# Transposes of the identity in TensorE's early waits, a higher count for x's sums in the planner, and one low part of the GLU on VectorE

## The chip, the cores and the metric

The kernel runs on one core of a Trainium2 chip. The metric is the device time of one execution in microseconds (us). TensorE (PE, with its weight loads PEld), VectorE (DVE), ScalarE (ACT) and GpSimd (POOL) each run their own queue in order; SyncE (SP) issues the DMAs.

## The reference

Three layers, in float32, over 2304 tokens of width 512:

```python
# 1. attention in chunks of 64 tokens, 8 heads of 64, softmax inside each chunk
out = softmax(q_c @ k_c.T / 8) @ v_c
# 2. x = that, heads joined; a mixture of 4 experts, F = 1024
p = domain_probs / (domain_probs.sum(-1, keepdims=True) + 1e-9)
out = sum(p[:, e:e+1] * (maximum(x @ w1[e], 0) @ w2[e]) for e in range(4))
# 3. RMS norm, then a gated unit, d_ff = 1536
xn = x / sqrt(mean(x * x) + 1e-6) * rms_g
g, val = xn @ w_gate, xn @ w_val
out = (g * sigmoid(g) * val) @ w_out
```

## The kernel before

**Tiling.** The 2304 tokens are three sets of 768; a set is two blocks of 384, a block three tiles of 128. For each layer and set the kernel walks over the feed-forward width in "outers" of two chunk pairs (`fps`, `UF = 2`). A number is held as a rounded high part and a low part, and each product is three passes (high by high, high by low, low by high). The first products (`hidden`) go by a Strassen-Winograd scheme: seven products over blocks, with sums of blocks of x (operands 4, 5, 6, 2, made by `x_sum`) and sums of blocks of the weights. Each operand is split by `x_parts`: ScalarE rounds the high part, VectorE (or GpSimd for operand 3) subtracts to get the low part. The products' sums are made on VectorE from PSUM (`u2`, `u3` and the adds into `c` and `d`).

**A GLU chunk.** `hidden` calls `use(b, j, ps)` four times, for (1,1), (0,0), (1,0) and (0,1), block b and column half j. `val_use` multiplies on VectorE, rounds `hi` on ScalarE (L734), and puts the low part's subtraction into `later`; `catch_up` issues it soon after, for (0,1) of an outer's second chunk as the first thing that `outer` does. `outer` then multiplies: tile 0 of block 0 takes (0,0) and (0,1) of both chunks, in twelve matmuls, of which the twelfth reads the low part of (0,1); block 1 follows three tiles later. There are nine outers in the GLU, so eighteen chunks, and 72 of these subtractions.

**The start.** Before the main loops, `race` writes out an order for the first attention of set 0 (three `attention_unit`s), the splitting of x, the first two chunks' products with operands 0 and 1 (`begin`, two products each, with a ScalarE copy `p1` between them, L639), and the first weights (`weights`, the `spare` runner). Each runner yields the engine and the time that its next step costs by a hand-written count; `race` always takes the runner that can begin first by these counts, and the steps go into the engines' queues in that order. So the counts decide, for example, how many of ScalarE's roundings of x's sums stand in its queue ahead of `p1`. PSUM is eight banks, handed out first in, first out.

Of the kernel before, what the change touches and what calls it, by code (L numbers as in the profile page):

```python
# [8 lines left out]
F32 = mybir.dt.float32  # L9
# [9 lines left out]
P = 128  # L19
# [52 lines left out]
class Chains:  # L72
# [28 lines left out]
                if c in self.chains and self.clock >= c[2]:  # L101
                    self.step(c, busy)

    def race(self, runners, spare):

        self.rush, busy = True, {}

        def enter(gen, at, then):
            return [gen, next(gen), [at], then]

        def begin(r):
            need, back = r[1] or ({}, 1)
            return max([r[2][-min(back, len(r[2]))]] + [busy.get(e, 0.0) for e in need])

        state, spare = [enter(*r) for r in runners], enter(*spare)
        while state:
            r = min(state, key=begin)  # L120
            if begin(spare) + 0.2 < begin(r):
                r = spare
            t, need = begin(r), (r[1] or ({}, 1))[0]
            for e, us in need.items():
                busy[e] = t + us
            r[2].append(t + max(need.values(), default=0.3) + 0.1)
            try:
                r[1] = next(r[0])
            except StopIteration:
                state.remove(r)  # L130
                state += [enter(*n) for n in (r[3](r[2][-1]) if r[3] else ())]
        self.rush = False
        self.clock = max(self.clock, busy["PE"])
        return spare[0]
# [13 lines left out]
def fused_kernel(ctx, tc, qkv, probs, w12, wglu, gvec, out):  # L148
# [4 lines left out]
    nc = tc.nc  # L153
# [13 lines left out]
    UF = 2  # L167
# [13 lines left out]
    banks = Banks(psum, [f"b{n}" for n in range(8)])  # L181
    work = Chains()

    ident = const.tile([P, P], F32, name="ident")
# [9 lines left out]
    sub = lambda eng, o, a, b: eng.tensor_tensor(o, a, b, op=ALU.subtract)  # L194
# [65 lines left out]
    def fetched():  # L260
        while not raws:
            if work.rush:
                work.step(fetching)
            yield
        ts, t = raws.pop(0)
        yield from work.pause(t + 8 - work.clock)
        return ts

    def store(t, where, name):
        yield from work.pause(3)  # L270
        nc.sync.dma_start(out=where, in_=t.bitcast(F32))
        written.add(name)
        yield from work.pause(7)
        release(t)
# [10 lines left out]
    def w1_load(where, key):  # L285
        for n in ORDER:
            while not w1p.free() or (*key[2:], n) not in written:
                yield
            t = w1p.get(f"w1_{n}")
            nc.sync.dma_start(out=t.bitcast(F32), in_=where[:, n])  # L290
            users[id(t)] = 1
            parts[(*key, n)] = t
            yield

    def weights():

        for s in range(NSET):
            for e in range(E):
                for u in range(NF1 // 2 // UF):
                    own = range(u * UF, (u + 1) * UF)  # L300
                    for fp in own if s > 0 else ():
                        yield from w1_load(w1m[e][fp], ("moe", s, e, fp))

                    for order in () if s > 0 else (ORDER,) if (e, u) != (0, 0) else ((0, 1), (5, 4, 6, 3, 2)):
                        for fp in own:
                            key, where = ("moe", s, e, fp), w1m[e][fp]
                            if order[0] == 0:
                                kept[fp] = yield from fetched()

                            def stored(n, t, key=key, where=where):  # L310
                                users[id(t)] = 2
                                parts[(*key, n)] = t
                                work.add(store(t, where[:, n], (*key[2:], n)))

                            yield from operands(kept[fp], w1p, stored, order)
                            if order[-1] == ORDER[-1]:
                                tp.put(*kept.pop(fp))
                    for f in range(2 * UF * u, 2 * UF * (u + 1)):
                        raw, = yield from fetched()
                        while not w2p.free():  # L320
                            yield
                        t = w2p.get("w2")
                        nc.scalar.copy(t[:, 0], raw)  # L323
                        yield
                        sub(nc.gpsimd, t[:, 1], raw, t[:, 0].bitcast(F32))
                        tp.put(raw)
                        parts["w2", "moe", s, e, f] = t
                        yield
        for s in range(NSET):
            for u in range(NF2 // 2 // UF):  # L330
                for fp in range(u * UF, (u + 1) * UF):
                    for g in range(2):
                        yield from w1_load(wgv[fp][g], ("glu", s, -1 - g, fp))
                for f in range(2 * UF * u, 2 * UF * (u + 1)):
                    while not w2p.free() or (f, 1) not in written:
                        yield
                    t = w2p.get("w2")
                    nc.sync.dma_start(out=t.bitcast(F32), in_=wou[f])
                    parts["w2", "glu", s, 0, f] = t
                    yield  # L340
# [216 lines left out]
    xs = {}  # L557
# [6 lines left out]
    def x_part(n, k):  # L564
        if n in tmp:
            return tmp[n][k][:, :NB]
        b, kd = x_at[n]
        return xr[:, b, kd + k, :]

    def x_sum(n):  # L570

        for o, *_ in x_made.get(n, ()):
            tmp[o] = [tp.get(f"s{o}_{k}") for k in range(KH)]
        for k in range(KH):
            for o, a, b, op in x_made.get(n, ()):
                yield {"DVE": 0.55}, 1
                op(nc.vector, x_part(o, k), x_part(a, k), x_part(b, k))

    def x_sums():
# [5 lines left out]
    def x_parts(n, eng, halves=False):  # L585

        t = xsp.tile([P, 2, KH, NB], F32R, tag=f"x{n}", name=f"x{n}")
        xs[n] = t
        if n in x_at and not halves:
            b, kd = x_at[n]  # L590
            pieces = [(slice(None), xr[:, b, kd:kd + KH, :])]
        else:
            pieces = [(k, x_part(n, k)) for k in range(KH)]
        for k, src in pieces:
            yield {"ACT": 0.5}, 1
            nc.scalar.copy(t[:, 0, k], src)
        for k, src in pieces:
            yield {"DVE": 0.55} if eng is nc.vector else {"POOL": 1.0}, len(pieces)
            sub(eng, t[:, 1, k], src, t[:, 0, k].bitcast(F32))

    def x_done():
        for n in list(tmp):
            tp.put(*tmp.pop(n))
# [15 lines left out]
    later, begun = [], {}  # L619
# [10 lines left out]
    def begin(key, use):  # L630

        yield {"PE": 1.2}, 1
        while not ((*key, 0) in parts and (*key, 1) in parts):
            yield {}, 1
        a = bank("a_ps")
        product(a, weight((*key, 0)), 0, True, False)
        yield {"ACT": 0.5}, 1
        p1 = cp.get("p1")
        nc.scalar.copy(p1, a[:, :NB])  # L639
        yield {"PE": 1.2}, 1  # L640
        product(a, weight((*key, 1)), 1, False, True)
        yield {"ACT": 0.5}, 1
        use(0, 0, a)
        yield {"DVE": 0.6}, 1
        catch_up()
        begun[key] = p1
# [80 lines left out]
    def val_use(fp):  # L727
        def use(b, j, ps):
            m = silu.pop((b, j))
            v = m[:, :NB]  # L730
            nc.vector.tensor_tensor(v, ps[:, :NB], v, op=ALU.mult)  # L731
            banks.put(ps)
            hi, lo = hh.get("hh"), hl.get("hl")
            nc.scalar.copy(hi, v)  # L734

            def rest():
                sub(nc.gpsimd, lo, v, hi.bitcast(F32))
                tp.put(m)

            later.append(rest)  # L740
            hs[fp, b, j] = (hi, lo)

        return use
# [80 lines left out]
    with tc.manual_schedule():  # L824
# [11 lines left out]
        nc.sync.dma_start(out=pr, in_=probs)  # L836
        nc.sync.dma_start(out=gb, in_=gvec.partition_broadcast(P))

        def one_block():
            yield from x_parts(0, nc.vector, True)  # L840
            yield from x_parts(1, nc.vector, True)
            for fp in range(UF):
                yield from begin(("moe", 0, 0, fp), moe_use(fp))
# [7 lines left out]
        def two_blocks(t):  # L851
            engines = {5: nc.vector, 4: nc.vector, 6: nc.vector, 3: nc.gpsimd, 2: nc.vector}
            return [(operand(n, eng), t + 0.8 * m, None) for m, (n, eng) in enumerate(engines.items())]

        gen = work.race(
            [
                (first[0], 4.4, None),
# [1 line left out]
                (first[2], 12.0, two_blocks),  # L859
            ],  # L860
            (weights(), 15.0, None),
        )
        x_done()
        feeding = work.add(gen, 0.5)
        nc.vector.tensor_reduce(psm, pr, axis=AX.X, op=ALU.add)
# [4 lines left out]
        for kind, s in [(kind, s) for kind in ("moe", "glu") for s in range(NSET)]:  # L870
            moe = kind == "moe"
# [128 lines left out]
```

## Time and profile before

| | |
|---|---|
| time, three runs | 1282.87 us median (1282.1 to 1284.8) |
| the profiled execution | 1280.6 us, span 1278.7 us |
| mean granted TensorE clock | 0.992 |
| busy share of the span | PE 96%, PEld 87%, DVE 62%, ACT 32%, POOL 44% |

TensorE is busy nearly all of the time, so the time is TensorE's work plus its idle stretches: 1278.7 less 1223.9 us. A row of a timeline gives the start, the time from the first start to the last end of the merged instructions, the engine, the line, the operation, and in brackets the idle time before it with what released it. The column PEclk is the granted TensorE clock as a share of 2.4 GHz; 0.50 is 1.2 GHz.

### The profile page before, as it was taken

The page shows a single profiled execution, that of the slowest core. Times are in us where ns is not written, and L with a number is a line of the kernel's source. Part 1 is how long each engine was busy: PE and PEld are TensorE (multiplying, and loading weights), DVE is VectorE, ACT ScalarE, POOL GpSimd, SP SyncE. Part 2 cuts the span into 40 slices and gives each one's busy share as a digit, 9 for nine tenths or more (in the row PEclk, how much of TensorE's full clock was granted, in tenths as well). Part 3 has the DMA queues.
Part 4 walks back from the last instruction along what each step waited for, and adds up shares of the span by engine and source line. Part 5 has one row for each costly group of instructions (what it writes and reads, how often), then busy time and mean ns, then how long its engine had stood idle before and what let it go on. Part 6 is the DMA issues. An engine that isn't in the chain of part 4 may idle for free. (4 is left out here: it accounts for less than half of the span.)

```text
span 1278.7 us, 20405 instructions
## 1 busy us (share of the span) xinstructions
PE 1223.9 (96%) x7200; PEld 1106.2 (87%) x7200; DVE 797.6 (62%) x1375; ACT 413.5 (32%) x924; POOL 562.6 (44%) x593
## 2 busy tenths in 40 slices
PE   6799999999987999999999999999999999999998
PEld 5588999989877888989998999897988988988997
DVE  6844344456766887667678666894758525763544
ACT  4434333333225232224232223243424232232211
POOL 5557676664345373527255255374305102132211
PEclk9899999999999999999999999999999999999999
DMA  8656555556577587655676777556856746755843
GB/s 285 219 169 218 190 191 187 184 185 209 191 250 241 165 296 264 208 191 210 239 251 207 256 239 243 169 195 258 288 162 225 266 126 217 255 193 195 280 141 122
DMA packets 139781, 274.29 MB, mean 215 GB/s; under 512 B 15648, under 2 KB 15648, under 8 KB 139680
## 3 DMA queue, kind: packets, MB, share of 16 engines
q1 hardware_dynamic: 139680, 272.99, 62.8%
q8 instruction: 57, 0.93, 0.3%
q14 instruction: 44, 0.36, 0.1%
HBM read 210.54 MB, written 62.39 MB: 213 GB/s over the span
## 5 line engine op out<-in xcount | busy, mean ns | idle before, releaser
L757 PE MATMUL o<-w,hh 128*128 128x512 f32 x1584 | 492.7, 392 | 4.0 <-ACT hh L697 2.2
L757 PEld LDWEIGHTS o<-w,hh 128*128 128x128 f32 x1584 | 295.9, 188 | 67.6 <-ACT hh L697 3.8
L757 PE MATMUL o<-w,hl 128*128 128x512 f32 x792 | 310.5, 392 | 8.4 <-POOL hl L194 8.4
L611 PE MATMUL a_ps<-x,w 128*128 128x384 f32 x1008 | 204.7, 339 | 12.1 <-ACT p L639 8.3
L611 PE MATMUL d_ps<-x,w 128*128 128x384 f32 x1008 | 203.9, 338 | 9.9 <-DVE c_ps L195 9.9
L194 POOL TENSOR_TENSOR w<-r,w 128x512 fp32r<-128x512 f32 (+1 forms) x144 | 162.4, 1138 | 104.8 <-ACT w L323 40.9
L611 PE MATMUL c_ps<-x,w 128*128 128x384 f32 x1008 | 203.7, 338 | 0.0
L194 POOL TENSOR_TENSOR hl<-silu,hh 128x384 fp32r<-128x384 f32 x72 | 73.5, 1049 | 283.3 <-ACT hh L734 282.1
L611 PEld LDWEIGHTS a_ps<-x,w 128*128 128x128 f32 x1008 | 178.2, 189 | 16.3 <-ACT p L639 9.0
L757 PEld LDWEIGHTS o<-w,hl 128*128 128x128 f32 x792 | 149.1, 188 | 44.6 <-POOL hl L194 12.2
L611 PEld LDWEIGHTS d_ps<-x,w 128*128 128x128 f32 x1008 | 176.2, 188 | 13.1 <-DVE c_ps L195 12.1
L611 PEld LDWEIGHTS c_ps<-x,w 128*128 128x128 f32 x1008 | 177.1, 189 | 0.2
L916 DVE SCALAR_TENSOR_TENSOR acc<-o,pr,acc 128x512 f32<-128x512 f32 x126 | 94.4, 749 | 126.3 <-PE o L757 126.2
L195 POOL TENSOR_TENSOR w<-w,sc 128x512 f32<-128x512 f32 x36 | 47.7, 1324 | 186.0 <-DVE sc L382 168.1
L194 POOL TENSOR_TENSOR w<-tw,w 128x256 fp32r<-128x256 f32 x112 | 90.2, 813 | 50.1 <-ACT w L227 50.1
L195 DVE TENSOR_TENSOR u<-b_ps,p 128x384 f32<-128x384 f32 x84 | 46.6, 554 | 96.5 <-PE b_ps L611 86.9
L611 PE MATMUL b_ps<-x,w 128*128 128x384 f32 x504 | 102.3, 339 | 0.0
L697 ACT ACTIVATE hh<-c_ps 128x384 fp32r<-128x384 f32 x96 | 47.3, 493 | 159.1 <-DVE c_ps L195 158.9
L195 DVE TENSOR_TENSOR u<-c_ps,u 128x384 f32<-128x384 f32 x84 | 46.7, 556 | 82.4 <-PE c_ps L611 82.0
L659 ACT COPY p<-a_ps 128x384 f32<-128x384 f32 x82 | 39.2, 478 | 167.6 <-PE a_ps L611 167.6
L611 PEld LDWEIGHTS b_ps<-x,w 128*128 128x128 f32 x504 | 89.3, 190 | 0.1
L227 ACT CAST w<-tw 128x256 fp32r<-128x256 f32 x112 | 42.5, 406 | 139.5 <-POOL tw L194 90.4
(95 smaller groups left out, 1311.2 us busy)
## 6 DMA issues: line engine op xcount, KB each, us to landing
w<-wgv SPq DMA_DIRECT2D x252, 256.0 KB, 4.1
w<-w1m SPq DMA_DIRECT2D x224, 256.0 KB, 5.2
r<-in_w SPq DMA_DIRECT2D x128, 256.0 KB, 4.7
w1m<-w SPq DMA_DIRECT2D x112, 256.0 KB, 2.2
wgv<-w SPq DMA_DIRECT2D x84, 256.0 KB, 4.5
raw<-in_wglu SPq DMA_DIRECT2D x36, 512.0 KB, 3.8
w<-wou SPq DMA_DIRECT2D x36, 512.0 KB, 7.5
wou<-q SPq DMA_DIRECT2D x24, 256.0 KB, 4.0
```

What stands on the lines that cost most here:

```text
L194: sub = lambda eng, o, a, b: eng.tensor_tensor(o, a, b, op=ALU.subtract)
L195: add = lambda eng, o, a, b: eng.tensor_tensor(o, a, b, op=ALU.add)
L227: nc.scalar.copy(halves(out[n])[:, 0], at[part_of[n]])
L611: nc.tensor.matmul(ps[:, :NB], wv[:, wi, k, :], xs[n][:, xi, k, :], start=(first and k == 0 and m == 0), stop=(last and k == KH - 1 and m ...
L659: nc.scalar.copy(p1, v(a))
L697: nc.scalar.activation(hi, src, AF.Relu)
L757: nc.tensor.matmul(ps, hs[fp, b, j][hx][:, r * P:(r + 1) * P], w2[2 * k + j][:, wi], start=((k, j, m) == (0, 0, 0)), stop=((k, j, m) == last),
L916: nc.vector.scalar_tensor_tensor(out=acc[i], in0=ps, scalar=pr[:, i, e:e + 1], in1=acc[i], op0=ALU.mult, op1=ALU.add,)
```

## The change

Three edits. (1) While `race` writes out the order, a bank `scratch` is held, and wherever TensorE's next step begins later by the plan than the last one ends, the gap divided by 0.13 us, rounded down, is issued as that many 128x128 float32 transposes of the identity into that bank. Once, when the runner `one_block` has ended, the rest up to its planned end is filled as well. (2) In the plan a VectorE sum or subtraction of x counts 0.85 us and not 0.55, a GpSimd one 1.1 and not 1.0. (3) In `val_use` the low part of (b, j) = (0, 1) is subtracted on VectorE and not on GpSimd.

```diff
-    def race(self, runners, spare):
+    def race(self, runners, spare, idle, until):
...
             t, need = begin(r), (r[1] or ({}, 1))[0]
+            if "PE" in need and "PE" in busy:
+                idle(t - busy["PE"])
             for e, us in need.items():
                 busy[e] = t + us
...
             except StopIteration:
                 state.remove(r)
+                if until():
+                    idle(r[2][-1] - busy["PE"])
+                    busy["PE"] = max(busy["PE"], r[2][-1])
...
             for o, a, b, op in x_made.get(n, ()):
-                yield {"DVE": 0.55}, 1
+                yield {"DVE": 0.85}, 1
...
-            yield {"DVE": 0.55} if eng is nc.vector else {"POOL": 1.0}, len(pieces)
+            yield {"DVE": 0.85} if eng is nc.vector else {"POOL": 1.1}, len(pieces)
...
-                sub(nc.gpsimd, lo, v, hi.bitcast(F32))
+                sub(nc.vector if b == 0 and j == 1 else nc.gpsimd, lo, v, hi.bitcast(F32))
...
+        early = [("moe", 0, 0, fp) for fp in range(UF)]
...
+        scratch = banks.get("scratch")
+        waited = []
+        def idle(us):
+            for _ in range(int(us / 0.13)):
+                nc.tensor.transpose(scratch[:, :P], ident, ident)
+        def until():
+            if 5 in xs and all(key in begun for key in early) and not waited:
+                waited.append(True)
+                return True
...
+            idle,
+            until,
         )
+        banks.put(scratch)
```

## Rows read from the trace of the kernel before

**Rows 1.** The page, busy time of TensorE, share of the span, instructions.
```profile
PE 1223.9 (96%) x7200; PEld 1106.2 (87%) x7200; DVE 797.6 (62%) x1375; ACT 413.5 (32%) x924; POOL 562.6 (44%) x593
```
**Rows 2.** Waits of TensorE: waiting, released by: total us, times, the longest.
```profile
PE o L757 <- POOL hl L194: 8.4, 9, 2.9
```
**Rows 3.** Timeline, all engines, the third outer of the GLU.
```profile
975.15 3.93 POOL L194 TENSOR_TENSOR hl<-silu,hh 128x384 fp32r<-128x384 f32 x4 [10.68 <-ACT hh L734]
...
976.57 0.56 DVE L731 TENSOR_TENSOR silu<-d_ps,silu 128x384 f32<-128x384 f32 x1
...
977.16 0.51 ACT L734 CAST hh<-silu 128x384 fp32r<-128x384 f32 x1 [0.55 <-DVE silu L731]
...
977.75 0.71 PE L757 MATMUL o<-w,hh 128*128 128x512 f32 x2
...
979.14 0.50 PE L757 MATMUL o<-w,hl 128*128 128x512 f32 x1 [0.68 <-POOL hl L194]
```
**Rows 4.** Timelines of GpSimd, ScalarE and TensorE, the first outer of the GLU.
```profile
876.36 1.18 POOL L194 TENSOR_TENSOR w<-w,w 128x256 fp32r<-128x256 f32 x1
877.50 2.58 POOL L194 TENSOR_TENSOR hl<-silu,hh 128x384 fp32r<-128x384 f32 x2
...
875.94 0.51 ACT L734 CAST hh<-silu 128x384 fp32r<-128x384 f32 x1 [0.65 <-DVE silu L731]
...
880.13 0.50 PE L757 MATMUL o<-w,hl 128*128 128x512 f32 x1 [2.90 <-POOL hl L194]
```
**Rows 5.** Timelines of VectorE and GpSimd near 831 and 1121 us.
```profile
831.45 0.95 DVE L194 TENSOR_TENSOR x<-xr,x 128x768 fp32r<-128x768 f32 x1
...
1120.64 1.46 DVE L194 TENSOR_TENSOR x<-xr,x 128x768 fp32r<-128x768 f32 x1 [1.32 <-ACT x L596]
...
1120.27 1.01 POOL L194 TENSOR_TENSOR hl<-silu,hh 128x384 fp32r<-128x384 f32 x1
```
**Rows 6.** Line 194: duration in ns, shortest, median, longest; first and last start.
```profile
L194 DVE TENSOR_TENSOR x<-s,x x28: 545/884/1753, 40.6 to 1129.4; 128x384 fp32r<-128x384 f32 x28
```
**Rows 7.** Timeline of TensorE, the first 60 us.
```profile
16.01 2.08 PE L540 MATMUL pv<-aT,v 64*64 64x64 f32 x62 [0.16 <-ACT aT L524]
20.50 1.30 PE L519 MATMUL trA<-ident,at 128*128 128x128 f32 x8 [2.41 <-POOL at L503]
...
22.47 3.18 PE L540 MATMUL pv<-aT,v 64*64 64x64 f32 x62 [0.17 <-ACT aT L524]
25.59 1.09 PE L519 MATMUL trA<-ident,at 128*128 128x128 f32 x8
...
27.41 2.08 PE L540 MATMUL pv<-aT,v 64*64 64x64 f32 x62 [0.16 <-ACT aT L524]
...
41.43 2.29 PE L611 MATMUL a_ps<-x,w 128*128 128x384 f32 x6 [6.79 <-ACT p L639]
43.52 2.08 PE L611 MATMUL b_ps<-x,w 128*128 128x384 f32 x6
...
48.94 1.31 PE L611 MATMUL d_ps<-x,w 128*128 128x384 f32 x6 [0.21 <-DVE c_ps L195]
```
**Rows 8.** Timelines of TensorE near 13 and 364 us: transposes.
```profile
13.75 0.47 PE L519 MATMUL trA<-ident,at 128*128 128x128 f32 x1
...
364.21 1.05 PE L519 MATMUL trA<-ident,at 128*128 128x128 f32 x4
```
**Rows 9.** Windows of 1 us: TensorE busy and count, PEclk, DMA share, GB/s.
```profile
22.00:23.00 1.00, 0.83 (x12) 0.50 0.89 199
...
39.00:40.00 1.00, 0.00 (x0) 0.50 0.00 0
```
**Rows 10.** Timelines of ScalarE and VectorE, 34 to 46 us.
```profile
40.91 0.47 ACT L639 COPY p<-a_ps 128x384 f32<-128x384 f32 x1
...
37.12 1.07 DVE L194 TENSOR_TENSOR s<-s,xr 128x384 f32<-128x384 f32 x1
...
40.58 4.96 DVE L194 TENSOR_TENSOR x<-s,x 128x384 fp32r<-128x384 f32 x8
```

## The prediction on record

> **What bounds the kernel.** The page first: TensorE is busy for 1223.9 of 1278.7 us [rows 1], so 54.8 us are idle, and a change pays only where it closes idle time of TensorE, or gives it back its high clock level, at a place where nothing else is late right behind. The list of TensorE's waits says where: nine waits for GpSimd's low part `hl`, 8.4 us in all, each in the GLU [rows 2], and in the start one of 6.79 us for ScalarE's `p1` [rows 7]. Then the timelines of these two places. In the GLU the reader is to see a chain of VectorE product, ScalarE rounding and GpSimd subtraction at the head of each outer, and that GpSimd does four subtractions in a row there [rows 3]. In the start TensorE's long waits lie between 18 and 41 us, and work behind them runs at the low level: the same 62 matmuls take 3.18 us at 22.47 and 2.08 us at 16.01 and 27.41, and a product of six takes 2.08 us at 43.52 [rows 7]; the granted clock reads 0.50 there, that is 1.2 of 2.4 GHz [rows 9]. After 48.94 us TensorE hardly pauses.
>
> **The low part on VectorE.** Take the third outer. The product on VectorE ends at 976.57 + 0.56 = 977.13, ScalarE's rounding at 977.16 + 0.51 = 977.67. GpSimd began its four subtractions at 975.15 and makes one in 3.93 / 4 = 0.98 us, so the last starts at 978.1 and ends at 979.08, and TensorE's twelfth matmul starts at 979.14; without a wait it would follow the pair of 977.75 after some 0.46, at 978.21 [rows 3]. On VectorE the subtraction is queued right behind the product and can start at 977.71, when VectorE has nothing else. Alone it takes 0.55 us (545 ns, the shortest of the same shape with both inputs in SBUF) [rows 6].
>
> But GpSimd is then in its third subtraction, from 977.11 to 978.13, and the two engines take turns. A VectorE subtraction of two SBUF operands took 0.95 us when it began before GpSimd's, and 1.46 us when it began at 1120.64 inside a GpSimd instruction that lasted until 1121.28: its own 0.95 us fits from 1121.15 to its end at 1122.10, so it waited until 0.13 us before the recorded end [rows 5]. Ours waits to 978.00, ends at 978.55, and TensorE goes on 0.06 later, at 978.61: 0.53 us saved. Eight outers show this pattern with the same wait (0.67 to 0.69 us): 8 x 0.53 = 4.2 us. Bounds: without the turn it ends at 978.26, 0.82 saved, 6.6 us in all; if it starts only at 978.13 and takes the median 884 ns [rows 6], TensorE goes on at 979.07, 0.6 us in all. I take 4.2, as the row inside a GpSimd instruction is the nearest.
>
> The first outer is another case: GpSimd mixes weights in, and its last two subtractions run from 877.50 to 880.08 [rows 4]. On VectorE ours is ready after ScalarE's 875.94 + 0.51, at 876.49; GpSimd holds an instruction from 876.36 that takes 0.74 us undisturbed (half the rows of its kind), so ours starts at 876.97, ends at 877.52, and TensorE goes on at 877.58 instead of 880.13 [rows 4]: 2.55 us. Bounds 2.1 (a VectorE sum beside a busy GpSimd took 1.07 [rows 10]) and 3.0 (no turn).
>
> What is late next: the low part of (1,0), still on GpSimd, is wanted three tiles, 36 matmuls, later; it ends before 979.1, so nothing. Behind the new instruction on VectorE stand the decoding of weights (first outer), x's low parts (last outer of a set) or nothing; they start 0.5 to 1.1 us later, and TensorE wants them a whole outer later. For the nine other chunks the subtraction stands ahead of `u2` of the next gate chunk, which waits for `p1` and a product anyway; I cost it at nothing, and it would be 0.5 us each, 4.5 us, if VectorE had no gap there. Sum for this edit: 4.2 + 2.55 = 6.7 us, bounds 2.7 to 9.6.
>
> **The new counts.** Stepping `race` by its own rule with 0.85 and 1.1: on ScalarE `p1` and the activation of the first chunk move ahead of all the roundings of the sums, and the second chunk's `p1` ahead of those of operands 6 and 2. In the old order `p1` stood behind them and ended at 41.38, just before TensorE's long wait ended [rows 7, 10]. In the new one it stands behind the second half of operand 5, whose sum ends on VectorE at 37.12 + 1.07 = 38.2 [rows 10], so it ends at some 39.3 and that chunk's second product runs two us earlier. Yet the next product, with operand 5, needs that operand's low parts, and VectorE is full from 29.5 to 47 us either way: it now does them third and fourth after the sums, by about 42. And the next wait is VectorE's again: `d` at 48.94 waits for `c`, behind the last x parts and the sums [rows 7]. So this edit alone moves 48.94 by only a few tenths; VectorE loses its one gap of 0.34 us ahead of `u3`.
>
> **The transposes.** Stepping the plan gives gaps of 1.4, 0.6, 0.95, 3.3, 0.95, 1.15, 3.5, 0.7, 1.75, 0.75 and 1.7 us, hence 10, 4, 7, 25, 7, 8, 26, 5, 13, 5 and 13 transposes, 123 in all. At the high level eight take 1.09 us [rows 7] and one 0.273, so (1.09 - 0.27) / 7 = 0.117 us each, 14.4 us in all; at the low level four take 1.05 and one 0.47, so 0.19 each [rows 8]. They stand in the queue ahead of real work. If they hold the level: the 25 after 18.09 us end at 21.0, 0.5 later than `trA` starts now; the second `pv` then runs in 2.08 instead of 3.18 [rows 7], net 0.6 us for x's tiles. The 14 among the scores lie before this: at 0.19 they are 2.7 us, partly inside waits for q and k, and I leave 1 us of loss for them in the range. After the third `pv` (ends 29.1) come 62 transposes and four products of 1.04: 29.1 + 7.3 + 4.2 = 40.6, with the wait for `p1` 42 at most, when operand 5 is ready; `b` runs at 42 instead of 43.52 and at the high level, and VectorE holds `d` to some 48.4. I take 0.5 us gained for edits 1 and 2 together. Bounds: 2.5 gained (0.6, and 1.9 for two products at 2.1 us [rows 7] if VectorE kept up); the loss is the second rival.
>
> One rule speaks against the transposes. What the rows show: the level was low at the first transpose (0.47 us at 13.75) and high by 16.01 [rows 7, 8]; in between TensorE did little but eight transposes, so they did not keep the level from rising, which bears out weakly that they count. The Trainium skill, "TensorE: Matmul & The Clock Gate", section "Part 4: PE-mode transpose", says that transpose mode does not count as busy for the clock in the same way and that the full level does not engage for it. By that rule the sum would be the second rival's and not a gain of 7.2 us.
>
> **The rivals.** *The transposes do not hold the level, and delay the work.* The long pause from 34.6 us let the level fall by 39 [rows 9]; if 62 transposes with four products between them count for as little, each is 0.19 and each product 2.08: `pv` late by 1.4 (ends 30.9), 26 x 0.19 = 4.9, then 4 x 2.08 + 36 x 0.19 = 15.2, so `b` starts at 51.0 instead of 43.52. TensorE is then the bound; `b`, `d`, `c`, `c` follow, two of them low, and `d` of 48.94 comes at 57.2: 8.3 us lost, 6.7 won in the GLU, 1282.87 + 1.6 = 1284.5. It decides for slower (2.6 us) from 9.3 lost at the start. For it: the pause's fall, and transposes placed in nearly every gap; against it: the rise at 13.75 to 16.01.
>
> *VectorE pays back what GpSimd gives.* The subtraction is slow beside GpSimd and nothing is won in the eight outers but 0.6: 0.6 + 2.1 + 0.5 = 3.2, 1279.7. For it: VectorE's median of 884 ns; against it: the rows behind 1120.64.
>
> *No turn to wait for:* 6.6 + 3.0 + 0.5 = 10.1, 1272.8. For it: VectorE's products with one PSUM operand beside GpSimd keep 0.56 [rows 3]; against it: both operands lie in SBUF here.
>
> **The numbers.** The profiled execution took 1280.6 us, 2.3 below the median of the three; 6.7 + 0.5 = 7.2 off makes 1273.4 for it and 1282.87 - 7.2 = 1275.7 for the median. Chances: forecast 0.50, first rival 0.28, second 0.10, third 0.12. The forecast's own range is 1272.5 to 1279 (GLU 4 to 9, start 1 lost to 2.5 gained). The first rival's goes from 1279 (the level holds in part) to 1290; leaving its upper third and the third rival's lower part out gives 1272.3 to 1285. What a measurement tells from no change is 0.2%, 2.6 us: below 1280.3 or above 1285.4. Faster: nearly all of the forecast and of the third, 0.07 of the first, 0.06 of the second, 0.73; slower 0.11, out of the first; same 0.16.
>
> **What would show it.** Right: 7323 matmuls; granted clock 1.00 from 20 to 48 us; the wait list's `hl` row down from 8.4 to about 3 us, named by VectorE; `b` near 42, `d` near 48.4. Wrong: 0.50 behind the transposes, 0.19 us apiece, `b` after 45; `hl` on VectorE at 0.9 us or more; new waits for `u` or `c` behind the nine first chunks.

## The result, and the profile after

The changed kernel takes 1271.94 us (median of four, 1270.46 to 1273.03), before 1282.48: the ratio is 0.9916, 95% interval 0.9900 to 0.9932, so some 10.8 us are gained where 7.2 were predicted. The time lies 0.36 us below the low end of the stated range. The profiled execution took 1270.46 us (span 1268.7, mean granted clock 0.997), 10.1 less than the one of before. One execution of the transposes alone, below, took 3145 us and is left out of every figure.

The page of the changed kernel, busy times [rows 1], and its list of TensorE's waits [rows 2] (total us, times, the longest):

```profile
PE 1230.4 (97%) x7323; PEld 1114.3 (88%) x7323; DVE 809.8 (64%) x1393; ACT 413.0 (33%) x924; POOL 544.5 (43%) x575
```

```profile
PE d_ps L617 <- DVE c_ps L201: 9.8, 9, 2.8
...
PE a_ps L617 <- ACT p L645: 3.6, 1, 3.6
PE trA L525 <- POOL at L509: 3.2, 2, 2.5
...
PE o L763 <- DVE hl L200: 0.3, 1, 0.3
```

The 123 transposes and the 18 moved subtractions are there (7200 to 7323; VectorE 1375 to 1393, GpSimd 593 to 575). The row for `hl` falls from 8.4 us in nine waits to 0.3 in one, but this is not all that is left: the weight loads (PEld) have rows of their own, for GpSimd's `hl` 12.2 us in nine waits before, for VectorE's 5.3 in nine after. So all nine are still there, 6.9 us shorter together.

**The GLU.** The timeline of the changed kernel, third outer, all engines [rows 3]:

```profile
968.80 2.98 POOL L200 TENSOR_TENSOR hl<-silu,hh 128x384 fp32r<-128x384 f32 x3 [11.82 <-ACT hh L740]
...
970.80 0.51 ACT L740 CAST hh<-silu 128x384 fp32r<-128x384 f32 x1 [0.55 <-DVE silu L737]
...
971.35 0.84 DVE L200 TENSOR_TENSOR hl<-silu,hh 128x384 fp32r<-128x384 f32 x1 [0.58 <-ACT hh L740]
...
971.39 0.70 PE L763 MATMUL o<-w,hh 128*128 128x512 f32 x2
...
972.24 0.50 PE L763 MATMUL o<-w,hl 128*128 128x512 f32 x1
```

VectorE's subtraction is issued 0.04 after the rounding ends and is recorded with 0.84 us, not the 0.55 that it takes alone: it ends at 972.19, while GpSimd's third ends at 971.78. That is the turn of the prediction, with its very size (0.55 + 0.29). From the pair of `hh` to the twelfth matmul it is now 0.85 us, in [rows 3] 1.39: 0.54 saved, and 0.39 more than the 0.46 that it would take without a wait (in eight outers 3.1 us, the "about 3" of the prediction). The same group over the whole GLU (count: shortest, median, longest in ns) and the first outer [rows 4]:

```profile
L200 DVE TENSOR_TENSOR hl<-silu,hh x18: 544/834/1305, 858.5 to 1250.0; 128x384 fp32r<-128x384 f32 x18
```

```profile
873.49 1.03 DVE L200 TENSOR_TENSOR hl<-silu,hh 128x384 fp32r<-128x384 f32 x1 [0.58 <-ACT hh L740]
...
874.58 0.50 PE L763 MATMUL o<-w,hl 128*128 128x512 f32 x1 [0.33 <-DVE hl L200]
```

In the first outer the waiting matmul moves from 880.13 to 874.58, of which 2.98 were there at the outer's first matmul already (874.08 to 871.10): 2.57 saved, 2.55 forecast. From the start of that outer's first matmul to that of the kernel's last it is 393.42 us, before 400.54: 7.1 for the GLU, 6.7 forecast.

**The start.** Timelines of TensorE and of ScalarE in the changed kernel [rows 7, 10]:

```profile
17.54 2.95 PE L868 MATMUL scratch<-ident 128*128 128x128 f32 x25
20.62 1.23 PE L525 MATMUL trA<-ident,at 128*128 128x128 f32 x8
21.69 0.93 PE L868 MATMUL scratch<-ident 128*128 128x128 f32 x7
22.55 2.08 PE L546 MATMUL pv<-aT,v 64*64 64x64 f32 x64
...
41.04 1.31 PE L617 MATMUL a_ps<-x,w 128*128 128x384 f32 x6 [3.57 <-ACT p L645]
42.18 2.86 PE L868 MATMUL scratch<-ident 128*128 128x128 f32 x13
44.69 1.76 PE L617 MATMUL b_ps<-x,w 128*128 128x384 f32 x6
...
49.87 1.29 PE L617 MATMUL d_ps<-x,w 128*128 128x384 f32 x6 [0.30 <-DVE c_ps L201]
```

```profile
38.25 0.41 ACT L233 CAST w<-tw 128x256 fp32r<-128x256 f32 x1 [2.87 <-POOL tw L200]
38.56 0.92 ACT L602 CAST x<-s 128x384 fp32r<-128x384 f32 x2
...
40.52 0.47 ACT L645 COPY p<-a_ps 128x384 f32<-128x384 f32 x1
```

The second `pv` runs in 2.08 us where it took 3.18 [rows 7]. But `p1` runs from 40.52 to 40.99 and does not end at some 39.3: the queue of ScalarE stands for 2.87 us at a rounding of weights that waits for GpSimd, and four roundings of sums and one more of weights come between that and `p1`. So `b` comes at 44.69 (before 43.52, forecast 42), behind the 13 last transposes, and `d` at 49.87 (before 48.94, forecast 48.4). The start itself is 0.9 us later. Nevertheless the first outer of the GLU is 2.98 earlier. The profiles differ at three later places: after 62 us the level falls before and not after (from 57.54 and 58.45, the first `o` of each, to the next product it takes 23.82 and 22.27 us); near 362 us `trA` waits 3.26 and 2.46; right behind it the level falls before [rows 8, the transposes of 364.21] and not after. That is 1.55 + 0.8 + 1.5, less the 0.9.

Only the 0.8 is there in every profile. The two falls of the level come and go. Near 62 us the level falls in two of the six profiles without transposes in the start, and in one of the seven with them; behind the `trA` wait near 362 us in five of the six and in four of the seven. The transposes behind that wait in the changed kernel, and in one that differs from it in the GLU alone (below, the low part of (1,0) on VectorE too):

```profile
362.15 0.60 PE L525 MATMUL trA<-ident,at 128*128 128x128 f32 x4
```

```profile
361.65 1.05 PE L525 MATMUL trA<-ident,at 128*128 128x128 f32 x4
```

So of the 2.98 us some 3 are two falls that this profile of before has and this one of the changed kernel hasn't, by chance as far as the profiles tell.

The windows of the changed kernel (columns: us, busy share and count of PE, PEld, DVE, ACT, POOL, then the granted clock, DMA share and GB/s; [rows 9]):

```profile
18.00:19.00 1.00, 1.00 (x11) 1.00 (x10) 1.00 (x3) 0.23 (x1) 1.00 (x2) 1.00 1.22 358
...
21.00:22.00 1.00, 1.00 (x10) 0.84 (x9) 0.93 (x4) 1.00 (x4) 0.45 (x2) 1.00 0.01 4
22.00:23.00 1.00, 1.00 (x20) 0.83 (x20) 0.50 (x3) 0.78 (x2) 1.00 (x3) 1.00 0.68 184
38.00:39.00 1.00, 0.00 (x0) 0.00 (x0) 0.63 (x2) 0.75 (x3) 1.00 (x2) 1.00 0.01 2
43.00:44.00 1.00, 1.00 (x7) 1.00 (x6) 1.00 (x3) 0.27 (x1) 0.27 (x1) 0.50 0.98 289
```

From 17.54 to 22.55 TensorE does nothing but 40 transposes (32 of the identity and the eight `trA` of the attention), and the clock is at 1.00 all through and behind them. In the start it falls only behind the wait of 3.57 us that the transposes don't fill, and the 13 that come then run partly at the low level.

### The profile page after: what moved, and what is told of

The parts are those of the page before. It is cut to its first block, busy times and chain, and to the rows that moved or that the text cites. A ratio compares the mean times of both kernels' runs of the same rounds, so it can differ in the third digit from the quotient of the medians.

```text
span 1268.7 us, 20615 instructions
## 1 busy us (share of the span) xinstructions
PE 1230.4 (97%) x7323; PEld 1114.3 (88%) x7323; DVE 809.8 (64%) x1393; ACT 413.0 (33%) x924; POOL 544.5 (43%) x575
## 5 line engine op out<-in xcount | busy, mean ns | idle before, releaser
L200 POOL TENSOR_TENSOR hl<-silu,hh 128x384 fp32r<-128x384 f32 x54 | 55.0, 1043 | 292.0 <-ACT hh L740 291.0
```

## The experiments

Gains are 1 minus the ratio, times the median of the kernel before in the same session; intervals are 95%.

**The low part alone** (before, with this edit):

```diff
-                sub(nc.gpsimd, lo, v, hi.bitcast(F32))
+                sub(nc.vector if b == 0 and j == 1 else nc.gpsimd, lo, v, hi.bitcast(F32))
```

> Only the low part of (0,1) on VectorE; no transposes, old counts. Theory A (the parts add up): the GLU's nine outers give what the two traces show between the first and the last outer, 7.1 us, and nothing else moves, so about 1275.4 against 1282.5, ratio 0.9945; the wait for hl falls from 8.4 to under 1 us; the stretches at the low clock level near 22, 42, 62 and 363 us stay as before. Theory B (the GLU edit alone makes all of the 10.5 us, the start is neutral): about 1272, ratio 0.992.

Measured: 1273.04 us, ratio 0.9922 (0.9908 to 0.9936), 10.0 us gained (8.2 to 11.8). Its profile reaches the GLU when before does (874.06 and 874.08) and takes 393.36 us from there, 7.2 less. The lion's share of the change is this edit. The time is theory B's (0.992; the interval leaves out theory A's 0.9945), the GLU of the profile is theory A's: the median gains more than the profiles show.

**The start alone** (the changed kernel, all low parts back on GpSimd):

```diff
-                sub(nc.vector if b == 0 and j == 1 else nc.gpsimd, lo, v, hi.bitcast(F32))
+                sub(nc.gpsimd, lo, v, hi.bitcast(F32))
```

> Only the transposes and the new counts; all low parts on GpSimd as before. Theory A: what is left of the 10.5 us, some 3.4 off, ratio 0.9975, although TensorE reaches the first d product later (49.9 instead of 48.9 us), because the stretches at the low level near 62 and 363 us go away for good. Theory B: those stretches come and go by chance from run to run, so on the median the start gives nothing or loses up to 1 us, ratio 0.999 to 1.001.

Measured: 1279.69 us, 0.9976 (0.9967 to 0.9985), 3.1 gained (1.9 to 4.2). Its profile has `b` at 45.21 and `d` at 50.53, later than before, and the GLU at 871.69, earlier by 2.4: as in the changed kernel, `d` is not earlier, the `trA` wait is shorter, and the level falls neither near 62 nor near 362 us. The time is theory A's, but its reason, that these two falls go away for good, doesn't hold: other kernels with these transposes have them (above).

**The counts alone** (before, with the three new counts):

```diff
-                yield {"DVE": 0.55}, 1
+                yield {"DVE": 0.85}, 1
...
-            yield {"DVE": 0.55} if eng is nc.vector else {"POOL": 1.0}, len(pieces)
+            yield {"DVE": 0.85} if eng is nc.vector else {"POOL": 1.1}, len(pieces)
```

> Only the new counts in the plan, no transposes. If the order alone helps: p1 of the second chunk leaves ScalarE before the roundings of operands 6 and 2, its second product runs near 40.5 us, operand 5's product starts near 42 instead of 43.5, and the first d that waits for VectorE comes near 48.6; 0.3 us off, ratio 0.9998. If the transposes are what counts and the order is neutral: the level is low from 39 to 45 us as before and the ratio is 1.000. If the order makes the whole gain of the start: 3 us off, ratio 0.9975.

Measured: 1281.25 us, 0.9984 (0.9974 to 0.9993), 2.1 gained (0.9 to 3.3), between the first two forecasts and the third (0.9975). In its profile the start is worse than anywhere (`d` at 52.05), the `trA` wait near 362 is 2.45 us, and in the first outer of the GLU the level falls behind the wait for `hl`. Windows of this kernel there (columns as above; in before the window from 882 reads 1.00):

```profile
881.00:882.00 1.00, 1.00 (x5) 0.82 (x6) 0.97 (x2) 0.62 (x2) 1.00 (x2) 1.00 0.54 205
882.00:883.00 1.00, 1.00 (x5) 0.77 (x4) 0.21 (x1) 0.73 (x3) 1.00 (x2) 0.61 0.55 209
883.00:884.00 1.00, 1.00 (x4) 0.81 (x3) 0.00 (x0) 0.25 (x1) 1.00 (x2) 0.50 0.24 90
```

Its GLU takes 402.24 us, 1.7 more than that of before (400.54), with the same instructions and the same wait of 2.90 us. So a wait that costs nothing in one execution costs 1.7 us of low level in another.

**The transposes alone** (before, with `idle`, `until` and the scratch bank, old counts; by these the gaps of the plan are others, and 115 transposes fill them, not 123):

```diff
+            if "PE" in need and "PE" in busy:
+                idle(t - busy["PE"])
...
+                if until():
+                    idle(r[2][-1] - busy["PE"])
+                    busy["PE"] = max(busy["PE"], r[2][-1])
```

> Only the transposes, with the old counts. Theory A (they keep the clock high, which is worth more than the places they take): the granted clock reads 1.00 from 15 to 40 us, operand 5's product starts no earlier than before, and the time is 2 to 3 us under the kernel before, ratio 0.998. Theory B (their effect is nothing beyond chance, the order of the new counts gives the gain): ratio 1.000.

Measured: 1281.6 us, 0.9984 (0.9970 to 0.9998), 2.1 gained (0.3 to 3.8). The profile is of a further execution:

> The transposes with the old counts once more, for a profile, as that of the first was of a disturbed execution. If they hold the level: granted clock 1.00 from 15 to 38 us, and the stretch up to the GLU takes 871 to 872 us as with both edits of the start. If the order of the new counts matters: the wait of 3.2 us near 362 stays, where the new counts have 2.45.

1281.71 us in that one execution. The level is 1.00 from 15 to 41 us, `b` comes at 43.48, `d` at 48.64; the `trA` wait near 362 is the old one, 3.2 us, so its 0.8 us belong to the counts. But the stretch up to the GLU takes 873.52 us and not 871 to 872: the level falls near 283, 362 and 396 us in spite of the transposes in the start. It falls again behind the `hl` wait of the first outer (GLU 402.22).

**Without the thirteen last transposes** (the changed kernel):

```diff
                 if until():
-                    idle(r[2][-1] - busy["PE"])
                     busy["PE"] = max(busy["PE"], r[2][-1])
```

> The changed kernel without the 13 transposes behind the second chunk's second product (the plan's TensorE time is still moved on). If they only stand in the way: operand 5's product starts near 42.2 us and not 44.7, the first d that waits for VectorE comes near 48.6 and not 49.9, 1.2 us off the changed kernel, about 1270.7. If VectorE bounds that place anyway: no difference, 1271.9. If they hold the level: low from 42 to 46 us in four products and not in one, 1 us slower than the changed kernel, 1273.

Measured: 1270.02 us, 0.9899 (0.9883 to 0.9914), 13.0 gained. In the profile `b` comes at 43.20, 1.5 earlier, but `d` at 49.85 as ever:

```profile
43.20 1.86 PE L616 MATMUL b_ps<-x,w 128*128 128x384 f32 x6
...
49.85 1.28 PE L616 MATMUL d_ps<-x,w 128*128 128x384 f32 x6 [1.67 <-DVE c_ps L200]
```

The 13 take a place in which TensorE would wait for VectorE's `c` anyway, here 1.67 us instead of 0.30. They are worth nothing that these runs can tell; the intervals with and without them overlap.

**The low part of (1,0) on VectorE too**, issued behind that of (0,1), so that GpSimd has only two subtractions:

```diff
+    held = []
...
-                sub(nc.vector if b == 0 and j == 1 else nc.gpsimd, lo, v, hi.bitcast(F32))
+                sub(nc.gpsimd if (b, j) in ((1, 1), (0, 0)) else nc.vector, lo, v, hi.bitcast(F32))
...
-            later.append(rest)
+            (held if (b, j) == (1, 0) else later).append(rest)
+            if (b, j) == (0, 1):
+                later.append(held.pop())
```

> The changed kernel with the low part of (1,0) on VectorE as well, behind that of (0,1), so that GpSimd has ended its two subtractions when VectorE starts. If VectorE's 0.84 us there is a turn behind GpSimd's third subtraction: 0.55 us now, the twelfth matmul of each outer starts 0.3 us earlier, 2.5 us off the changed kernel in nine outers, about 1269.5. If 0.84 us is what the subtraction costs in itself: no gain, and two of them ahead of the next gate chunk's sum cost up to 2 us, 1274.

Measured: 1268.75 us, 0.9888 (0.9868 to 0.9908), 14.4 gained (11.8 to 16.9), the lowest median of all, though its interval overlaps those of the next two. Its third outer:

```profile
968.77 2.00 POOL L200 TENSOR_TENSOR hl<-silu,hh 128x384 fp32r<-128x384 f32 x2 [13.66 <-ACT hh L742]
...
971.33 1.02 DVE L200 TENSOR_TENSOR hl<-silu,hh 128x384 fp32r<-128x384 f32 x2 [0.58 <-ACT hh L742]
...
971.37 0.70 PE L767 MATMUL o<-w,hh 128*128 128x512 f32 x2
...
971.94 0.50 PE L767 MATMUL o<-w,hl 128*128 128x512 f32 x1
```

With GpSimd idle from 970.77, two subtractions take 1.02 us on VectorE, and the twelfth matmul comes 0.57 after the pair instead of 0.85. That is the turn taken away, 0.28 an outer; the GLU takes 391.22 us by the profile, 2.2 less than in the changed kernel.

**The same without the thirteen**:

> The changed kernel with both steps that measured faster: the low parts of (0,1) and (1,0) on VectorE, and without the last 13 transposes. If they add up: 3.2 and 1.9 us off the changed kernel, about 1267, ratio 0.988. If leaving out the 13 gains nothing beyond chance: as with both low parts alone, 1268.8, ratio 0.9888.

Measured: 1270.17 us, 0.9897 (0.9879 to 0.9916). No gain over the version with them.

**The same with the counts, but no transposes at all**:

> The low parts of (0,1) and (1,0) on VectorE and the new counts, but no transposes at all. If the transposes are worth 1 to 2 us beside the counts: 1270 to 1271, ratio 0.990. If they are worth nothing: 1268.8, ratio 0.9888. Its profile has the low level in the first 50 us in any case.

Measured: 1273.62 us, 0.9920 (0.9904 to 0.9937), 10.3 gained: 2.9 less than with the transposes but for the thirteen (same session; the lowest of its six executions is 1272.03, the highest of the other's five 1272.38), 4.1 less than with all of them (another session). In the start TensorE has the same waits unfilled, and the level falls behind them; `d` comes at 51.13 instead of 49.16. Windows of this kernel (columns as above):

```profile
21.00:22.00 1.00, 0.00 (x0) 0.00 (x0) 0.97 (x4) 0.07 (x1) 0.58 (x2) 1.00 0.00 0
...
23.00:24.00 1.00, 0.80 (x7) 0.37 (x5) 0.93 (x3) 1.00 (x3) 0.83 (x2) 0.67 0.32 53
24.00:25.00 1.00, 1.00 (x18) 1.00 (x20) 0.04 (x1) 0.24 (x1) 1.00 (x3) 0.50 0.88 334
```

The second `pv` of this kernel, 2.08 us in the changed one:

```profile
23.43 3.88 PE L540 MATMUL pv<-aT,v 64*64 64x64 f32 x64
```

**Only the wait of the first outer filled** (before, with 24 transposes ahead of the twelfth matmul of the first GLU outer, nothing else):

```diff
-    def outer(fps, w2, flush, aside):
+    def outer(fps, w2, flush, aside, fill=0):
...
+                        if fill and (t, k, j, m) == (0, 1, 1, 2):
+                            pad = bank("pad")
+                            for _ in range(fill):
+                                nc.tensor.transpose(pad[:, :P], ident, ident)
+                            banks.put(pad)
...
-                outer(fps, w2, flush, aside)
+                outer(fps, w2, flush, aside, 24 if not moe and s == 0 and k == 0 else 0)
```

> The kernel before, with 24 transposes (2.8 us at the high level) in TensorE's wait ahead of the twelfth matmul of the GLU's first outer; the wait itself stays. Theory C (in most runs the level falls behind that wait, 1.7 us a time, as in the profile of the counts alone at 882 us; the edit on VectorE takes this away too, which is why it measured 10 us and not 7): no fall there, 1.3 us off on the median, ratio 0.999. Theory B (the fall is rare): ratio 1.000.

Measured: 1281.67 us, 0.9988 (0.9976 to 0.9999), 1.5 gained (0.1 to 3.1). The timeline of TensorE shows the wait filled and the waiting matmul no later:

```profile
875.68 0.73 PE L762 MATMUL o<-w,hh 128*128 128x512 f32 x2 [0.20 <-ACT hh L734]
876.25 2.78 PE L760 MATMUL pad<-ident 128*128 128x128 f32 x24
879.33 0.50 PE L762 MATMUL o<-w,hl 128*128 128x512 f32 x1 [0.30 <-POOL hl L194]
```

In the profile the GLU takes 400.62 us, the same as in that of before, which had no fall there. A gain in the median and none between the profiles fits a level that falls here in part of the executions; the lower end of the interval, 0.1, is close to no gain.

**Edit 3 in the first outer alone**:

```diff
-                sub(nc.gpsimd, lo, v, hi.bitcast(F32))
+                sub(nc.vector if (b, j) == (0, 1) and s == 0 and fp < UF else nc.gpsimd, lo, v, hi.bitcast(F32))
```

> The kernel before, with the low part of (0,1) on VectorE in the two chunks of the GLU's first outer only. Without a fall of the level: 2.6 us off, ratio 0.998. With theory C, 2.6 + 1.3 = 3.9 us off, ratio 0.997. If the first outer carries all that e1 measured beyond the trace's 7.1 us: 5.7 us off, ratio 0.9956.

Measured: 1277.1 us, 0.9951 (0.9931 to 0.9971), 6.3 gained (3.7 to 8.8); by the profile the GLU is 2.44 shorter. The eight other outers are the rest to the low part alone, 10.0 - 6.3 = 3.7, near 8 x 0.53 = 4.2, but by the two intervals it is uncertain by some 3 us. What the medians give beyond the profiles belongs to the first outer, or to both kernels by chance.

**Transposes in the second attention** (the version without the thirteen, and 34 more, meant for the waits near 362 and 400 us):

```diff
+            if u[0] == 12 and a == 0:
+                pad = banks.get("pad")
+                for _ in range(18):
...
+        if u[0] == 14:
+            pad = banks.get("pad")
+            for _ in range(16):
```

> e9 with 18 transposes ahead of the first trA of set 2's attention (in its wait of 2.4 us near 360 us) and 16 ahead of the second unit's pv (in its wait of 2.1 us near 399). If transposes hold the level there as in the start: no low stretch near 363 us and none or a shorter one near 400, 1 to 2 us off e9. If the Trainium skill's rule holds, that transposes do not count: the same low stretches, and the time of e9.

Measured: 1274.02 us, 0.9919 (0.9896 to 0.9942), 3.9 more than without them. The instructions of that tile (count: shortest, median, longest in ns; first and last start) show why this says nothing of its question:

```profile
L525 PE MATMUL pad<-ident x18: 272/272/273, 331.5 to 333.4; 128*128 128x128 f32 x18
...
L546 PE MATMUL pad<-ident x16: 272/272/273, 368.3 to 370.0; 128*128 128x128 f32 x16
```

Both groups came some 30 us ahead of the waits that they were meant for, where TensorE has other work. If they only delayed it, that is 34 x 0.117 = 4.0 us by the duration of [rows 7]; 3.9 are measured, but the intervals of the two kernels overlap, so the agreement is partly luck. Whether filled waits near 362 and 400 us would pay stays open.

## Why the prediction was half right

Two terms of the sum failed by their size: the 2.55 us for the first outer of the GLU, measured 6.3 (3.7 to 8.8) alone, and "I take 0.5 us gained for edits 1 and 2 together", measured 3.1 (1.9 to 4.2) alone. Both were read from one profile; that other executions spend more time at the low level, and so have more to gain, was put at nothing.

**Edit 3: right in mechanism and, by the profiles, in size; too small for the median.** The turn behind GpSimd's subtraction (0.53 forecast, 0.53 to 0.55 in the eight outers), the first outer (2.55 and 2.57), VectorE paying nothing back (TensorE's waits for its `c_ps` are 9.9 us in all before and 9.8 after): 6.7 forecast, 7.1 in the profiles. The median of this edit alone gains 10.0 (8.2 to 11.8), which leaves 6.7 out. The third rival, no turn, gave nearly the measured time, by a mechanism that isn't there: VectorE's median is 834 ns, and taking GpSimd's third subtraction away brought 0.28 an outer more. The second rival is out, since it gave the eight outers 0.6 us together, and each of them gained 0.53 to 0.55.

**The start.** Its way was wrong: `p1` did not end at 39.3, since I passed over the rounding of weights ahead of it on ScalarE, which waits for GpSimd, and `d` came 0.9 later in the profile instead of 0.5 earlier. That 0.9 is itself a draw: four profiles whose start is that of before have `d` from 48.06 to 50.82, the six with both edits of the start from 49.01 to 50.53, the two with the counts and no transposes at 52.05 and 51.13. So the transposes win back in the start what the new counts lose there, one to two us, and against before nothing is gained up to `d`. Its size was wrong, 3.1 (1.9 to 4.2) alone: I had priced the level only in the first 50 us of one profiled execution. The mean granted clock of each timed execution shows how much more there was to win (us at the low level: (1 - clock) x span / 0.5, means over the executions):

| kernel | executions | mean us | mean clock | us at the low level |
|---|---|---|---|---|
| before, its profile alone | 1 | 1280.6 | 0.992 | 20 |
| before, beside the experiments | 56 | 1283.1 | 0.9883 | 30 |
| low part alone | 5 | 1273.2 | 0.9892 | 28 |
| counts alone | 12 | 1281.1 | 0.9899 | 26 |
| transposes alone | 11 | 1281.0 | 0.9921 | 20 |
| start alone | 11 | 1279.7 | 0.9945 | 14 |
| changed | 4 | 1271.8 | 0.9952 | 12 |
| both low parts, no transposes | 6 | 1273.6 | 0.9900 | 25 |
| both low parts, with transposes | 4 | 1269.4 | 0.9942 | 15 |

An average execution of before spends 30 us at the low level, not the 20 of its profile, and the changed kernel 12. (The half speed that the durations show in the first us, last section, is not in this clock.) Over the 56 executions of before a microsecond at the low level goes with 0.21 us of time (a fitted slope; part of the low level lies in waits): 16 us less, as in the start alone, are then 3.4 us by estimate, and 3.4 are the difference of the means. That the transposes cut the time at the low level is shown, by the windows and by these clocks (30 to 20 us alone, 26 to 14 beside the counts, 25 to 15 beside both low parts). That this is the time gained is the estimate above, not shown apart; and at which waits it is won in the executions without a profile is not shown either.

**First rival: out.** The transposes hold the level (17.54 to 22.55 us at 1.00), and filled waits have it where the unfilled ones lose it: in all seven profiles with transposes the second `pv` takes 2.08 us, in the six without 3.18 to 3.90. The Trainium skill, "TensorE: Matmul & The Clock Gate", section "Part 4: PE-mode transpose", says that transpose mode does not count as busy for the clock in the same way; for these float32 transposes the traces say otherwise, and the measurement decides.

**The missing term.** The wait of 2.9 us in the first outer costs more than itself: in two of the four profiles with this wait unfilled a fall follows (402.2 instead of 400.5 us), and filling it gave 1.5 us (0.1 to 3.1). So edit 3 can take away up to 1.7 us of low level as well. The GLU's 7.1, the start alone's 3.1 and this make 10.2 to 11.9 against 10.8 (8.7 to 12.8) measured. The clocks bear this term out only in part: against before in the same session the executions spend 28 us at the low level and not 31 where the wait is filled, 22 and not 31 with edit 3 in the first outer alone, which is more than one fall that costs 1.7 us can be, but 28 and 28 with the low part alone.

**The range.** The forecast's own range is narrower than its terms: 9 for the GLU and 2.5 for the start give 1282.87 - 11.5 = 1271.4, not 1272.5, and 1271.94 lies above that. And where the prediction's part on the transposes speaks of the second rival, the loss is that of the first in its list.

**What stays open.** The low part alone gained 10.0 us (8.2 to 11.8), of which the profiles and the fall explain 7.2 to 8.9; in the first outer alone they explain 2.4 to 4.1 of 6.3 (3.7 to 8.8). The counts alone gained 2.1 us (0.9 to 3.3), although they delay `d`; the `trA` wait explains 0.8 of it. And how the counts make the `trA` wait near 362 us 0.8 shorter: it is 2.4 to 2.5 in every profile with the new counts and 3.2 to 3.3 in every one with the old; in between GpSimd's `at` starts a little sooner, but what moved it wasn't followed.

## What to carry to other kernels

One profile shows one draw of the clock: look at the mean granted clock of all timed executions before pricing it, and count each long wait of TensorE as its own length plus the chance of a low stretch behind it. Filling such a wait with transposes of a constant cost nothing here where they ended before the wait did (24 of them, the waiting matmul no later), and gained 1.5 us where full work followed; put into a place where TensorE doesn't wait, they delay it, by about their length in the one kernel that shows it. A subtraction of two SBUF operands that TensorE waits for was worth moving from GpSimd to VectorE even beside a busy GpSimd (0.84 us there against 0.98); moving its neighbour away from GpSimd too brought 0.28 us an outer more.

## What the hardware showed unexpectedly

- The same order of instructions with the same wait of 2.90 us has a fall of the clock behind it in one execution and none in another (GLU of 402.2 and 400.5 us).
- Transposes hold the full speed (40 of them in a row, above), and bring it sooner. In the first 7 us the granted clock reads 1.00 in every kernel, but the durations are those of half speed. With ten transposes at 7.56 us, 16 score matmuls take 0.41 us from 12.59 on; in the kernel with both low parts and no transposes they still take 0.71 then. It is so in all seven profiles with transposes (the last scores 0.41 to 0.46) and in all six without (0.70 or 0.71). Timelines of TensorE, the changed kernel and that one:

```profile
7.56 2.39 PE L868 MATMUL scratch<-ident 128*128 128x128 f32 x10
...
12.59 0.41 PE L468 MATMUL sc<-qk_b 64*64 64x64 f32 x16
```

```profile
12.42 0.71 PE L462 MATMUL sc<-qk_b 64*64 64x64 f32 x16
13.46 1.97 PE L519 MATMUL trA<-ident,at 128*128 128x128 f32 x8 [0.34 <-POOL at L503]
```

  So where the clock column can't tell, the duration of a known shape does.
- VectorE's subtraction beside GpSimd's: 0.84 us, and two in 1.02 us when GpSimd had stopped.
